# A small piece of w_q on 24 partitions in place of 16, and the last eight steps of w_o in their own order

## The chip, the cores and the metric

The kernel runs on one core of a Trainium2 chip. The metric is the time of one execution on the device, in microseconds (us). A core has TensorE (PE; its weight loads are listed apart as PEld), VectorE (DVE), ScalarE (ACT), GpSimd (POOL), SyncE (SP, which here only issues transfers), and 16 DMA engines that carry every transfer between HBM and the on-chip memory.

## The reference

One decode step of a transformer block for two tokens (B = 2, D = 448), everything in float32:

```python
xn = layernorm(x)
q  = xn @ wq                                  # 448 x 4096: 16 heads of 256
s  = softmax(q k^T / 16) v                    # 8 KV heads x 2 batches, 4096 cached positions each
s  = s.reshape(B, 1, 4096) @ wo               # 4096 x 448
g  = silu(((xn @ w_gate) * (xn @ w_up)) @ w_down)
out = x + s * g
```

The caches are 134 MB and the weights about 24 MB; each byte is read once, and there are only two tokens to use it on.

## The kernel before, in words

**Streaming.** A (KV head, batch) pair is one step i = 0..15. Its keys are a [128, 8192] float32 array and so are its values, 4 MB each. `issue` (L63 to L81) sends loads in a fixed order on SP's queue, and the order was laid down by the `plan` calls (L86 to L94): w_q's first half, k0, then for each step a pair "values of step i, keys of step i+1" (8 MB), with the other weights between them. Keys and values go to a ring of two 8 MB buffers, weights to one slot. SP waits until the buffer to be overwritten has been used, so the ring holds TensorE and the DMA queue together.

**Computing.** For step i, `values` (L282) multiplies the probabilities with v_i, `scores` (L238) makes the scores of step i+1, `softmax` (L258) turns them into probabilities. TensorE uses its array as four column blocks of 32, so that one matmul has 32 output rows and four run side by side. Float32 matmuls show as two records each in the profile, and as many weight loads.

**w_q's short end.** D = 448 is 3 x 128 + 64. The first three blocks of 128 rows are full. Of the last 64 rows, half of the columns lie on partitions 64 to 127 of the slot's block 12 (L184), and the other half is a separate array, `wqx`: 64 rows of 2 x 512 columns. Before, it is folded into 4 groups (NK) of 16 rows (SIDE), so it sits on 16 partitions with 4096 columns each, 256 KB. In HBM the 16 rows are 4 groups of 4 with an unused fifth row behind each group (L431). `rows` multiplies group j with `xeT[:, j]`, the matching 16 rows of the transposed x (L138 to L141, L178 to L181).

**The end of the kernel.** The output projection has 32 steps of 128 rows of w_o. 24 of them come earlier as a weight. The last 8 (LATE = 24) lie behind the last values in the array `last1`, in the order `THIRD` = 24, 25, 26, 28, 29, 30, 31, 27. `plan` at L94 cuts this array into eight transfers: 4096, 3072 and 1024 columns of v15, then w_o steps as 3 + 3 + 1 + 1/2 + 1/2 (a step is 448 columns; 224 KB over 128 partitions). Steps 24 to 27 multiply `oT1`, which is ready early; steps 28 to 31 multiply `oT2`, which exists only when the last two steps' outputs have been scaled (L390), combined (L391) and turned (L392). `project_last` (L323) does one step as four matmuls of 112 columns; step 27 is done in two halves of 56 columns, one per transfer. Then VectorE multiplies by the gate and adds x (L398, L399), and SP stores the result (L400).

Of the kernel before, what the change touches and what calls it, by code (L numbers as in the profile page):

```python
# [13 lines left out]
B, D = 2, 448  # L14
HKV, REP, SK, DH = 8, 2, 4096, 256
F = 1792
NT = 4
W = 32
DUP = W // 2
NK = 4  # L20
FC = F // NT
KB = 16
ROW = 8192
SL = D // NT
NC = HKV * 4
EARLY = 16
LATE = 24
THIRD = [24, 25, 26, 28, 29, 30, 31, 27]
PART = 14 * (D + 512)
SIDE = 16  # L30
EXTRA = 8
EPS = 1e-5


# [5 lines left out]
def gated_decode_block(ctx: ExitStack, tc: tile.TileContext, x, first, vk, last0, last1, wq0, wqx, wdq, wo, wgu, out):  # L40
    nc = tc.nc
# [11 lines left out]
    def bank(name=None):  # L53
        return psum.tile([128, 512], F32, name=name, bufs=1) if name else two()[:, 0]
# [4 lines left out]
    LAST = N - B  # L59
    loaded = {}  # L60
    todo = []

    def issue(n=1):  # L63
        for names, src, cuts in todo[:n]:
            weight = names[0].startswith("w")
            if weight:
                t = slot.tile([128, PART], F32, name="slot", align_bytes=512)
            else:
                t = ring.tile([128, 2 * ROW], F32, name="ring", align_bytes=512)
            width = ROW if not weight else src.shape[1] // len(names)  # L70
            for i, name in enumerate(names):
                loaded[name] = t[:, i * width:(i + 1) * width]
            if names == ["wd", "wq1"]:
                loaded["wd"], loaded["wq1"] = t[:, :14 * D], t[:, 14 * D:]
            for lo, hi in zip(cuts, cuts[1:]):
                nc.sync.dma_start(t[:, lo:hi], src[:, lo:hi])  # L76
            if names == ["wq0"]:
                at = src.shape[1]
                loaded["wqx"] = t[:, at:at + EXTRA * 512]
                nc.sync.dma_start(loaded["wqx"][:SIDE], wqx[:, :4])  # L80
        del todo[:n]  # L81

    def plan(names, src, cuts=None):
        todo.append((names.split(), src, cuts or [0, src.shape[1]]))
# [6 lines left out]
        if i in weights:  # L91
            plan(*weights[i])
    plan(f"k{LAST + 1} v{LAST}", last0, [0, ROW, 2 * ROW])
    plan(f"v{LAST + 1} wo2", last1, [0, 4096, 7168, *(ROW + i * D // 2 for i in (0, 6, 12, 14, 15, 16))])  # L94
    issue(3)


# [6 lines left out]
    ident = const.tile([128, 128], F32)  # L104
# [18 lines left out]
    xn = e1[:, 1]  # L123
    nc.vector.tensor_scalar(xn[:, :D], xc, rstd, None, op0=OP.mult)
    nc.vector.tensor_scalar(xn[:, D:], xc[:, 384:], rstd, None, op0=OP.mult)
    pt = bank()
# [5 lines left out]


    oT1 = const.tile([128, 3, 2, REP, W], F32)
    xeT = oT1[:SIDE].rearrange("p g d r m -> p (g d r) m")[:, :NK]
    pt = bank()
    for j in range(NK):
        at = 384 + j * SIDE  # L138
        nc.tensor.transpose(pt[:SIDE, B * j:B * (j + 1)], xn[:, at:at + SIDE], ident[:B, :B])
    nc.vector.tensor_copy(xeT.rearrange("p k (b j) -> p k b j", b=B),  # L140
                          pt[:SIDE, :NK * B].rearrange("p (k b) -> p k b", b=B)[:, :, :, None].to_broadcast([SIDE, NK, B, DUP]))  # L141

    both = work.tile([128, D], F32, name="h")[:B, :W].rearrange("p (b j) -> p b j", b=B)
    nc.vector.tensor_copy(both, ident[:B, :B, None].to_broadcast([B, B, DUP]))
    pt = bank()
    for c in range(NT):
        nc.tensor.matmul(pt[W * c:W * (c + 1), :SL], both.rearrange("p b j -> p (b j)"), x2[:, c * SL:(c + 1) * SL],
                         start=True, stop=True)
# [18 lines left out]
    def rows(ps, w, n, extra=None):  # L167


        def block(i):  # L170
            return w[:, i * n:(i + 1) * n]

        for k in range(3):
            for c in range(NT):
                nc.tensor.matmul(ps[W * c:W * (c + 1), :n], xnT[:, k, :], block(NT * k + c), start=k == 0, stop=False)  # L175
        if extra is not None:

            for j in range(NK):  # L178
                for c in range(2):
                    at = (c * NK + j) * n  # L180
                    nc.tensor.matmul(ps[W * c:W * (c + 1), :n], xeT[:, j, :], extra[:SIDE, at:at + n], start=False, stop=j == NK - 1)  # L181
                    if j == 0:
                        half = slice(64 * c, 64 * (c + 1))
                        nc.tensor.matmul(ps[W * (2 + c):W * (3 + c), :n], xnT[half, 3, :], block(12)[half], start=False, stop=True)  # L184
            return
        for c in range(NT):
            half = slice(0, 64) if c < 2 else slice(64, 128)
            nc.tensor.matmul(ps[W * c:W * (c + 1), :n], xnT[half, 3, :], block(12 + c % 2)[half], start=False, stop=True)
# [4 lines left out]
    def query(h):  # L193
        ps = bank()
        rows(ps, loaded[f"wq{h}"], 512, None if h else loaded["wqx"])
        for r in range(REP):
            nc.vector.transpose(qT[h][:, :, :, :, r, :].rearrange("p b g d j -> p (g d) b j"),  # L197
                                ps[:, r * 256:(r + 1) * 256])
# [16 lines left out]
    def ffn_in():  # L215
        pp = two()
        for i, w in enumerate(("wg", "wu")):
            rows(pp[:, i], loaded[w], FC)
        g = work.tile([128, FC], F32, name="h")
        nc.scalar.copy(g, pp[:, 0, :FC])  # L220
        h = work.tile([128, FC], F32, name="h")
        nc.vector.tensor_mul(h, pp[:, 1, :FC], g)
        nc.vector.transpose(hT.rearrange("p i m -> p (i m)"), h)
# [34 lines left out]
    def softmax(i, s, m, pT=None):  # L258
        sm = bank("sm")
        nc.tensor.transpose(sm[:1, :128], m[:, 0:1], ident)  # L260
        mx = work.tile([1, NT, W], F32, name="mx", bufs=1)
        nc.vector.tensor_reduce(  # L262
            mx, sm[:1, None, :128].rearrange("p o (c j) -> p o j c", c=NT).to_broadcast([1, NT, W, NT]),
            axis=AX.X, op=OP.max)
        nc.tensor.transpose(sm[:, 128:129], mx.rearrange("p c j -> p (c j)"), one)  # L265
        nc.vector.tensor_scalar(m[:, 1:2], sm[:, 128:129], -1.0 / 16, None, op0=OP.mult)  # L266
        p = work.tile([128, 2, 512], F32, name="p", bufs=1)
        nc.scalar.activation(p, s, AF.Exp, bias=m[:, 1:2], scale=1.0 / 16, accum_out=su[:, place(i):place(i) + 1])  # L268
        if pT is None:
            pT = work.tile([128, 2, 512], F32, name="pT", bufs=1)  # L270
        nc.vector.transpose(pT.rearrange("p h n -> p (h n)"), p.rearrange("p h n -> p (h n)"))  # L271
        return pT
# [38 lines left out]
    def turn(oT, cb, g, b, n):  # L311
        nc.vector.transpose(oT[:, g:g + n, :, :, DUP * b:DUP * (b + 1)].rearrange("p g d r j -> p (g d) r j"), cb)  # L312

    def heads(oT, i, first):
        return oT[:, i // 4 - first, i % 2, i % 4 // 2]
# [5 lines left out]
                             loaded["wo"][:, i * D:(i + 1) * D], start=i < NT, stop=i >= LATE - NT)  # L321

    def project_last(oT, first, i):  # L323

        at, last = THIRD.index(i) * D, i == THIRD[-1]
        cols = SL // 2 if last else SL
        for lo in range(0, SL, cols):
            for n in range(NT):
                nc.tensor.matmul(acc[W * n:W * (n + 1), lo:lo + cols], heads(oT, i, first),  # L329
                                 loaded["wo2"][:, at + n * cols:at + (n + 1) * cols], start=False, stop=last and lo > 0)  # L330
            at += NT * cols

    query(0)
    ob = work.tile([128, 8, 512], F32, name="ob", bufs=1)
# [4 lines left out]
    p = softmax(0, *ss)  # L339
    for i in range(LAST):  # L340
        g, b = divmod(i, B)
# [9 lines left out]
        p = softmax(i + 1, *ss)  # L351
# [19 lines left out]
    ps = [p]  # L371
# [3 lines left out]
    last = slot.tile([128, PART], F32, name="slot", align_bytes=512)  # L375
    p = softmax(LAST + 1, *ss, last[:, :1024].rearrange("p (h n) -> p h n", h=2))
    o = bank("o")
    values(LAST, ps[0], o)
    acc = bank()
# [10 lines left out]
    nc.scalar.activation(ob[:, 7], o, AF.Copy, scale=over[:, 15:16])  # L390
    cb = combine(ob[:, 7:], 1)  # L391
    turn(oT2, cb[:, :64], 0, 1, 1)  # L392
    for i in THIRD:
        project_last(*((oT2, 7) if i >= 28 else (oT1, 4)), i)

    r0 = work.tile([128, D], F32, name="h")[:, :SL]
# [55 lines left out]
```

## Time and profile before

| | us |
|---|---|
| median of 3 runs | 376.22 (376.15 to 376.42) |
| the profiled execution | 376.37 |
| its span, first to last instruction | 374.6 |
| DMA queue of SP, share of the 16 engines over the span | 98.2% |
| TensorE busy (matmul records) | 203.6 (54%) |
| VectorE busy | 72.6 (19%) |
| mean granted TensorE clock | 0.772 |

The profile's page gives busy times, a picture of the span in 40 slices, the DMA queues, and the chain of work that ended last. The DMA share of a stretch is the mean busy share of the 16 engines, so 0.0625 is one engine working alone. A packet's bytes are put down at its start, so that a share in a short stretch can go over 1.

### The profile page before, as it was taken

To read this page: it belongs to the slowest core of one execution; us is meant where nothing else is said; L and a number is where in the kernel's file an instruction comes from. 1 tells how busy PE (TensorE), PEld (TensorE's weight loads), DVE (VectorE), ACT (ScalarE), POOL (GpSimd) and SP (SyncE) were. 2 spreads that over 40 slices of the span, in tenths; PEclk is the share of its full clock that TensorE was granted. 3 is DMA by queue.
4 is the path that set the end of the run, shared out by engine and by line. 5 is a ranking of instruction groups with operands and counts; after the bars stand their busy time and mean duration, and the time that the engine had idled before them with its cause. 6 is when DMAs were issued, how large, how long until landed. Compare 5 with 4: busy or idle time off the path is not lost.

```text
span 374.6 us, 3200 instructions
## 1 busy us (share of the span) xinstructions
PE 203.6 (54%) x1446; PEld 57.3 (15%) x1446; DVE 72.6 (19%) x121; ACT 25.3 (7%) x39; POOL 1.2 (0%) x7
## 2 busy tenths in 40 slices
PE   1796458082734090857372665721819180909785
PEld 0111112020211020212020111200202020202222
DVE  4002130104040003040404041300120312040541
ACT  1000010001020002010101010100010101010120
POOL 1000000000000000000000000000000000000000
PEclk9956598768578577696768596885867687776999
DMA  8999899999999999999999999999999999999994
GB/s 327 432 500 441 374 432 448 448 436 435 419 442 441 441 441 400 422 448 450 420 441 434 443 415 409 457 441 434 450 420 422 441 434 427 436 409 441 413 416 178
DMA packets 4356, 158.78 MB, mean 424 GB/s; under 512 B 614, under 2 KB 1000, under 8 KB 1384
## 3 DMA queue, kind: packets, MB, share of 16 engines
q1 hardware_dynamic: 4340, 158.59, 98.2%
q8 instruction: 11, 0.18, 0.2%
q14 instruction: 1, 0.01, 0.0%
q10 hardware_dynamic: 4, 0.00, 0.0%
HBM read 158.54 MB, written 0.06 MB: 423 GB/s over the span
## 4 chain that ended last, share of the span: by engine, by line
DMA 74%; PE 24%; issue 1%; SPq 0%; DVE 0%
DMA ring<-vk 66%; PE o L286 11%; PE s L247 8%; DMA ring<-last 5%; DMA slot<-wq 3%; PE s L181 2%; PE s L175 1%; PE s L184 1%; PE s L329 0%; SPq L76 0%; PE sm L279 0%; DVE h L398 0%; DVE h L399 0%
## 5 line engine op out<-in xcount | busy, mean ns | idle before, releaser
L286 PE MATMUL o<-ring,pT 128*32 128x512 f32 x480 | 87.3, 893 | 112.4 <-DMA ring<-vk 112.4
L248 DVE TENSOR_REDUCE m<-s 128x1 f32<-128x1024 f32 x16 | 19.6, 1222 | 221.9 <-PE s L247 221.9
L247 PE MATMUL s<-ring,qT 128*32 128x512 f32 x512 | 60.7, 616 | 0.9 <-PE s L181 0.9
L286 PEld LDWEIGHTS o<-ring,pT 128*32 128x32 f32 x480 | 21.7, 155 | 167.8 <-issue 154.2
L268 ACT ACTIVATE p<-s,m 128x1024 f32<-128x1024 f32 x16 | 17.8, 1113 | 293.7 <-DVE m L266 293.7
L247 PEld LDWEIGHTS s<-ring,qT 128*32 128x32 f32 x512 | 17.5, 114 | 42.3 <-issue 39.7
L271 DVE STREAM_TRANSPOSE pT<-p 128x1024 f32<-128x1024 f32 x15 | 18.7, 1245 | 21.2 <-ACT p L268 21.2
L175 PE MATMUL s<-slot,xnT 128*32 128x512 f32 (+1 forms) x96 | 14.1, 733 | 7.3 <-DMA slot<-wq 4.3
L260 PE MATMUL sm<-ident,m 128*1 128x128 f32 x16 | 4.3, 270 | 18.8 <-DVE m L248 18.8
L265 PE MATMUL sm<-one,mx 1*128 1x1 f32 x16 | 3.5, 220 | 14.6 <-DVE mx L262 14.6
L262 DVE TENSOR_REDUCE mx<-sm 1x128 f32<-1x512 f32 x16 | 10.7, 670 | 2.1 <-PE sm L260 2.1
L347 DVE COPY ob<-o 128x512 f32<-128x512 f32 x14 | 9.5, 681 | 0.0
L181 PE MATMUL s<-slot,oT 16*32 16x512 f32 x16 | 7.4, 942 | 0.0
L320 PE MATMUL wide<-slot,oT 128*32 128x448 f32 x48 | 6.6, 699 | 0.6 <-DVE oT L312 0.6
L229 PE MATMUL s<-slot,hT 128*32 128x448 f32 x28 | 4.7, 786 | 3.4 <-DMA slot<-wdq 3.4
L260 PEld LDWEIGHTS sm<-ident,m 128*1 128x1 f32 x16 | 1.3, 79 | 33.0 <-DVE m L248 32.4
L175 PEld LDWEIGHTS s<-slot,xnT 128*32 128x32 f32 x96 | 3.6, 134 | 15.2 <-issue 15.2
L295 PE MATMUL cb<-ob,add_blocks 128*32 128x64 f32 (+2 forms) x64 | 4.3, 384 | 2.4 <-DVE ob L347 1.6
L197 DVE STREAM_TRANSPOSE qT<-s 128x256 f32<-128x256 f32 x4 | 1.6, 428 | 19.4 <-PE s L181 18.4
L265 PEld LDWEIGHTS sm<-one,mx 1*128 1x128 f32 x16 | 2.2, 136 | 17.6 <-DVE mx L262 17.6
L268 ACT ACT_TABLE_LOAD x2 | 2.6, 1283 | 27.4 <-DVE m L266 25.2
L286 PE MATMUL wide<-ring,slot 128*32 128x512 f32 x32 | 4.1, 597 | 0.0
(68 smaller groups left out, 46.8 us busy)
## 6 DMA issues: line engine op xcount, KB each, us to landing
ring<-last SPq DMA_DIRECT2D x2, 4096.0 KB, 24.1
slot<-wdq SPq DMA_DIRECT2D x1, 6720.0 KB
slot<-wgu SPq DMA_DIRECT2D x1, 6272.0 KB, 30.6
slot<-wo SPq DMA_DIRECT2D x1, 5376.0 KB, 41.9
ring<-first SPq DMA_DIRECT2D x1, 4096.0 KB, 21.0
slot<-wq SPq DMA_DIRECT2D x1, 3328.0 KB, 10.7
ring<-last SPq DMA_DIRECT2D x1, 2048.0 KB, 14.1
ring<-last SPq DMA_DIRECT2D x1, 1536.0 KB
```

The lines of the kernel that those rows point to most:

```text
L175: nc.tensor.matmul(ps[W * c:W * (c + 1), :n], xnT[:, k, :], block(NT * k + c), start=k == 0, stop=False)
L181: nc.tensor.matmul(ps[W * c:W * (c + 1), :n], xeT[:, j, :], extra[:SIDE, at:at + n], start=False, stop=j == NK - 1)
L247: nc.tensor.matmul(s[W * c:W * (c + 1), h, :], q[:, d], k[:, h, d, c, :], start=d == 0, stop=d == 1)
L248: nc.vector.tensor_reduce(m[:, 0:1], s, axis=AX.XY, op=OP.max)
L260: nc.tensor.transpose(sm[:1, :128], m[:, 0:1], ident)
L262: nc.vector.tensor_reduce(mx, sm[:1, None, :128].rearrange("p o (c j) -> p o j c", c=NT).to_broadcast([1, NT, W, NT]), axis=AX.X, op=OP.max)
L265: nc.tensor.transpose(sm[:, 128:129], mx.rearrange("p c j -> p (c j)"), one)
L268: nc.scalar.activation(p, s, AF.Exp, bias=m[:, 1:2], scale=1.0 / 16, accum_out=su[:, place(i):place(i) + 1])
L271: nc.vector.transpose(pT.rearrange("p h n -> p (h n)"), p.rearrange("p h n -> p (h n)"))
L286: nc.tensor.matmul(o[W * t:W * (t + 1), :], pT[:, h, at:at + 2 * W:2], loaded[f"v{i}"][:, e * 512:(e + 1) * 512], start=e < NT, stop=e >= ...
L320: nc.tensor.matmul(wide[W * t:W * (t + 1), :D], heads(oT, i, first), loaded["wo"][:, i * D:(i + 1) * D], start=i < NT, stop=i >= LATE - NT)
L347: nc.vector.tensor_copy(ob[:, place(i) % 8], o)
```

## The change

1. SIDE goes from 16 to 24 and the number of groups from 4 to 3 (`NS`). `wqx` is read onto 24 partitions with 2 x 3 x 512 = 3072 columns each; in HBM the 24 rows are 6 groups of 4 with an unused fifth behind each. 3 x 24 = 72 rows are 8 more than there are, and these are zeros: 288 KB are read, 256 KB are used. The transposes and matmuls on it go from 4 to 3 per column half, and the copy of the transposed x from PSUM becomes two copies (24 rows x 2 groups, 16 rows x 1 group).
2. `THIRD` is gone. Steps 24 to 31 lie and are done in their own order, each as four matmuls of 112 columns, and the array is cut into 4 + 1 + 1 + 1 + 1 steps.

```diff
-THIRD = [24, 25, 26, 28, 29, 30, 31, 27]
-SIDE = 16
-EXTRA = 8
+SIDE = 24
+NS = 3
+EXTRA = 2 * NS
...
-    plan(f"v{LAST + 1} wo2", last1, [0, 4096, 7168, *(ROW + i * D // 2 for i in (0, 6, 12, 14, 15, 16))])
+    plan(f"v{LAST + 1} wo2", last1, [0, 4096, 7168, *(ROW + i * D for i in (0, 4, 5, 6, 7, 8))])
...
-    xeT = oT1[:SIDE].rearrange("p g d r m -> p (g d r) m")[:, :NK]
+    xeT = oT1[:SIDE].rearrange("p g d r m -> p (g d r) m")[:, :NS]
     pt = bank()
-    for j in range(NK):
-        at = 384 + j * SIDE
-        nc.tensor.transpose(pt[:SIDE, B * j:B * (j + 1)], xn[:, at:at + SIDE], ident[:B, :B])
-    nc.vector.tensor_copy(xeT.rearrange("p k (b j) -> p k b j", b=B),
-                          pt[:SIDE, :NK * B].rearrange("p (k b) -> p k b", b=B)[:, :, :, None].to_broadcast([SIDE, NK, B, DUP]))
+    for j in range(NS):
+        lo, hi = 384 + j * SIDE, min(384 + (j + 1) * SIDE, D)
+        nc.tensor.transpose(pt[:hi - lo, B * j:B * (j + 1)], xn[:, lo:hi], ident[:B, :B])
+    for n, lo, hi in ((SIDE, 0, NS - 1), (64 - SIDE * (NS - 1), NS - 1, NS)):
+        nc.vector.tensor_copy(xeT[:n, lo:hi].rearrange("p k (b j) -> p k b j", b=B),
+                              pt[:n, lo * B:hi * B].rearrange("p (k b) -> p k b", b=B)[:, :, :, None].to_broadcast([n, hi - lo, B, DUP]))
...
-            for j in range(NK):
+            for j in range(NS):
+                n_rows = min(SIDE, 64 - j * SIDE)
                 for c in range(2):
-                    at = (c * NK + j) * n
-                    nc.tensor.matmul(ps[W * c:W * (c + 1), :n], xeT[:, j, :], extra[:SIDE, at:at + n], start=False, stop=j == NK - 1)
+                    at = (c * NS + j) * n
+                    nc.tensor.matmul(ps[W * c:W * (c + 1), :n], xeT[:n_rows, j, :], extra[:n_rows, at:at + n],
+                                     start=False, stop=j == NS - 1)
...
     def project_last(oT, first, i):
-
-        at, last = THIRD.index(i) * D, i == THIRD[-1]
-        cols = SL // 2 if last else SL
-        for lo in range(0, SL, cols):
-            for n in range(NT):
-                nc.tensor.matmul(acc[W * n:W * (n + 1), lo:lo + cols], heads(oT, i, first),
-                                 loaded["wo2"][:, at + n * cols:at + (n + 1) * cols], start=False, stop=last and lo > 0)
-            at += NT * cols
+        for n in range(NT):
+            at = (i - LATE) * D + n * SL
+            nc.tensor.matmul(acc[W * n:W * (n + 1), :SL], heads(oT, i, first), loaded["wo2"][:, at:at + SL],
+                             start=False, stop=i == NC - 1)
...
-    for i in THIRD:
+    for i in range(LATE, NC):
         project_last(*((oT2, 7) if i >= 28 else (oT1, 4)), i)
...
-    ends = wq0[:64, 12 * 512:].reshape(NK, SIDE // 4, 4, 2, 512).transpose(1, 2, 3, 0, 4)
+    ends = np.zeros((NS * SIDE, 2, 512), np.float32)
+    ends[:64] = wq0[:64, 12 * 512:].reshape(64, 2, 512)
+    ends = ends.reshape(NS, SIDE // 4, 4, 2, 512).transpose(1, 2, 3, 0, 4)
```

More of the change, by code (lines that the diff above doesn't have):

```diff
@@ L431 @@
     wqx = np.zeros((SIDE // 4, 5, EXTRA * 512), np.float32)
-    ends = wq0[:64, 12 * 512:].reshape(NK, SIDE // 4, 4, 2, 512).transpose(1, 2, 3, 0, 4)
+    ends = np.zeros((NS * SIDE, 2, 512), np.float32)
+    ends[:64] = wq0[:64, 12 * 512:].reshape(64, 2, 512)
+    ends = ends.reshape(NS, SIDE // 4, 4, 2, 512).transpose(1, 2, 3, 0, 4)
     wqx[:, :4] = ends.reshape(SIDE // 4, 4, EXTRA * 512)
     wq0 = np.concatenate([wq0[:, :12 * 512], np.concatenate([wq0[64:, 12 * 512:13 * 512], wq0[64:, 13 * 512:]])], 1)
-    wo = np.asarray(A_wo).reshape(NC, 128, D)[[*range(LATE), *THIRD]]
-    wo[-1] = wo[-1].reshape(128, NT, 2, SL // 2).transpose(0, 2, 1, 3).reshape(128, D)
+    wo = np.asarray(A_wo).reshape(NC, 128, D)
     wo = wo.transpose(1, 0, 2).reshape(128, NC * D)
```

## The prediction

> **What bounds the kernel now.** I read the page first: the picture of the span, the queues, the chain that ended last.
>
> ```profile
> span 374.6 us, 3200 instructions
> ...
> DMA  8999899999999999999999999999999999999994
> ...
> q1 hardware_dynamic: 4340, 158.59, 98.2%
> q8 instruction: 11, 0.18, 0.2%
> q14 instruction: 1, 0.01, 0.0%
> ...
> DMA 74%; PE 24%; issue 1%; SPq 0%; DVE 0%
> ```
>
> The 16 DMA engines are full from the first slice to the last. TensorE's share of the chain is only the moment at which a ring buffer comes free; by then the next load is queued already. Nothing that makes an engine faster in the middle can help; what counts is the bytes that each of the 16 engines has to carry, since a load has landed only when the slowest engine has brought its part. So the second view is the stages at the very end.
>
> ```profile
> core 0: us, PE busy (x) PEld busy (x) DVE busy (x) ACT busy (x) POOL busy (x), PEclk, DMA share, GB/s
> 362.00:364.00 2.00, 2.00 (x28) 0.84 (x22) 0.66 (x2) 0.00 (x0) 0.00 (x0) 1.00 0.99 419
> ...
> 368.00:368.40 0.40, 0.00 (x0) 0.00 (x0) 0.00 (x0) 0.40 (x1) 0.00 (x0) 1.00 0.75 300
> ...
> 369.20:369.60 0.40, 0.40 (x20) 0.20 (x10) 0.19 (x1) 0.00 (x0) 0.00 (x0) 1.00 0.47 170
> 369.60:370.00 0.40, 0.05 (x4) 0.00 (x0) 0.00 (x0) 0.00 (x0) 0.00 (x0) 1.00 0.37 128
> 370.00:370.20 0.20, 0.08 (x4) 0.11 (x8) 0.00 (x0) 0.00 (x0) 0.00 (x0) 1.00 0.19 67
> 370.20:370.80 0.60, 0.60 (x29) 0.60 (x31) 0.00 (x0) 0.00 (x0) 0.00 (x0) 1.00 0.07 22
> 370.80:371.00 0.20, 0.20 (x18) 0.13 (x12) 0.00 (x0) 0.00 (x0) 0.00 (x0) 1.00 0.02 4
> ```
>
> Times 16, the share counts the engines still working: 12 at 368.2, 7.5 at 369.4, 6 at 369.8, 3 at 370.1, and then 1.1. From 370.2 one engine works alone: 0.07 x 16 x 0.6 = 0.67 engine-us, of which it takes 0.60, so the second-last ended at about 370.27; in the last row 0.02 x 16 x 0.2 = 0.06, so the last ends at 370.86. It is 0.59 us behind the second-last, and four engines were done before 368. The last piece of w_o waits for this one engine.
>
> **What makes the engines unequal.** All large loads cover 128 partitions and give each engine the same. Three things do not: w_q's small piece, instruction code (q8, 11 packets of 16 KB) and the table packet (q14). How many engines share the piece can be counted in its stretch, and one packet of code can be priced.
>
> ```profile
> DMA packets 54, 1.02 MB, mean 462 GB/s; under 512 B 15, under 2 KB 15, under 8 KB 15
> ## 3 DMA queue, kind: packets, MB, share of 16 engines
> q1 hardware_dynamic: 54, 1.02, 107.4%
> ...
> q8 instruction: 1, 0.02, 1.1%
> ```
>
> The first three lines are the stretch 10.3 to 12.5 us, the last one 45 to 50 us. In the first, 54 - 15 = 39 packets carry data, of 16 KB (w_q's piece) or 32 KB (the first keys): 1.02 MB is 16 and 23 of them. So the piece is 16 packets, one per partition row. An engine moves 419 / (16 x 0.99) = 26.5 GB/s (the row of 362 us), so a 16 KB packet takes 0.62 us, and 16 packets that begin inside 2.2 us are about four engines with four packets each: four groups of four rows in HBM, four engines. Each of these carries 4 x 0.62 = 2.47 us more than the rest. A code packet costs 0.011 x 16 x 5 = 0.88 us on one engine. Followed packet by packet in the records (no view prints that), code falls on eight other engines, in turn, so that some get two; four engines have neither; the last engine is one of w_q's four, and the table packet is on it too.
>
> **The change, part 1: w_q's piece.** Six groups of four rows are, by the same pattern, six engines with four packets of 12,288 B. At 26.5 GB/s that is 0.464 us each, 1.85 us per engine: 0.62 less on the four, 1.85 more on two new ones. No row shows 24 partitions; the ends are four engines with six packets (2.78 us, 0.31 more than now) and eight engines with three (1.39). I take six, for the pattern of groups.
>
> By the Trainium skill ("DMA: Bandwidth & Descriptors", section on why a DMA increments its semaphore by 16) a transfer uses the largest number up to 16 that divides the slowest dimension on both sides, and the lowest-numbered engines: 4 of 4 and 16 before, 6 of 6 and 24 after. The count before agrees with the trace; no row here can show the numbers of the engines.
>
> The last engine then ends at 370.86 - 0.62 = 370.24, level with the second-last, which has no part in w_q and stays at 370.27. If the two new engines are among those that were done before 368, they end at 368 + 1.85 = 369.85 at the latest, and nobody waits for them. So of the 0.62 us, 0.59 reaches the end.
>
> The rest of part 1 costs nothing that counts; its cover is in these rows.
>
> ```profile
> 1.18 0.78 SPq L80 DMA_DIRECT2D slot<-wqx  x1
> 2.01 0.41 SPq L76 DMA_DIRECT2D ring<-first  x1
> 2.47 0.50 SPq L76 DMA_DIRECT2D ring<-vk  x1
> ...
> 6.21 0.27 DVE L140 COPY oT<-s 16x128 f32<-16x128 f32 x1
> ...
> 7.98 0.19 DVE L165 COPY add_blocks<-rows 128x64 f32<-128x64 f32 x1
> ...
> 11.57 4.91 PE L175 MATMUL s<-slot,xnT 128*32 128x512 f32 x24 [4.31 <-DMA slot<-wq]
> ...
> 21.16 5.33 PE L181 MATMUL s<-slot,oT 16*32 16x512 f32 x12
> ...
> 33.84 0.33 SPq L76 DMA_DIRECT2D ring<-vk  x1
> ```
>
> - VectorE: two copies for one, 0.27 us becomes at most twice that. VectorE is done at 8.2 and TensorE waits for w_q until 11.5; without that cover it would be 0.27 us.
> - SP: with six groups for four the issue may go from 0.78 to 1.17 us. The first keys, queued behind it, are issued 0.4 us later, at 2.4; the 3.4 MB of w_q ahead keep the engines busy until about 10.
> - TensorE: four of 16 records at L181 go, at 5.33 / 12 = 0.44 us: 1.8 us off the first query. The next ring load is then issued at 32.1, not 33.84. No gain: by 2.97 us SP has issued 3.4 + 0.3 + 4.2 + 8.4 = 16.3 MB, at 0.424 MB per us work until about 40. For the same reason a loss here of up to 6 us would cost nothing.
> - 32 KB more are read: in the 1.85 us already.
>
> **Part 2: the tail.**
>
> ```profile
> 365.70 2.15 PE L286 MATMUL wide<-ring,slot 128*32 128x512 f32 x16
> ...
> 368.64 0.43 PE L295 MATMUL cb<-ob,add_blocks 128*32 128x64 f32 x16 [0.79 <-ACT ob L390]
> ...
> 368.89 0.76 PE L329 MATMUL s<-ring,oT 128*32 128x112 f32 x24
> 369.14 0.25 DVE L312 STREAM_TRANSPOSE oT<-cb 128x64 f32<-128x64 f32 x1 [2.94 <-PE cb L295]
> ...
> 370.12 1.40 PE L329 MATMUL s<-ring,oT 128*32 128x112 f32 x48 [0.47 <-DMA ring<-last]
> 371.59 0.28 DVE L398 TENSOR_TENSOR h<-s,gate 128x112 f32<-128x112 f32 x1 [2.20 <-PE s L329]
> ```
>
> Transfers: five pieces of w_o before and after, eight rows of each on every engine, so 40 packets per engine either way, and the same bytes, so the last byte comes at the same time. SP issues the same number, the last two still behind a wait for earlier pieces, 13 us ahead of their data.
>
> TensorE: 72 records become 64. Steps 24 to 27 go first: 32 records at (0.76 - 0.26) / 23 = 0.022 us, from 368.89 to 369.8. Their piece is 4/3 as long, but four steps of 224 KB (8 x 1792 B per engine, 0.54 us) follow it, so it is complete at 370.27 - 2.2 = 368.1. Steps 28 to 31 need the turn that ends at 369.39, and one 224 KB piece each, at 0.54 us spacing; a step takes 8 x 0.022 = 0.18. So each waits for its piece, none for the one before, and none for the turn: step 30 would be done by 370.0 if all had landed. What comes after the last byte grows: eight records of 112 columns, 7 x 0.022 + 0.26 = 0.41 us, for eight of 56. The latter lie between nothing saved and half of it (0.21); the finish at 371.56, 0.70 after the last byte, leaves 0.3 for them if a landing is seen after 0.4. I take +0.08, bounds 0 and +0.2.
>
> [...]
>
> **The sum.** -0.59 + 0.08 = -0.51 us on the profiled 376.37: 375.86. The median was 0.15 below that execution, so the forecast for the median is 376.22 - 0.51 = 375.7, 0.14% less. A measurement of this kernel tells about 0.2% (0.75 us) from no change, so this counts as within it.
>
> **Rivals.**
>
> 1. *The two new engines are ones that carry code* (slower). Of the 12 engines at work at 368.2 the eight with code end, by the shares above, between 369 and 370.27. Plus 1.85: 370.9 to 372.1, up to 1.2 us past today's 370.86, and with 0.08 up to +1.3: 376.3 to 377.5. It decides as soon as one of the two ends after 369.0 today. For it: 8 of the 12 engines outside w_q's four carry code, and no view numbers the engines. Against it: eight engines in turn look like one half of the 16, and w_q's four lie outside it, so the next two should be in their half.
> 2. *Hidden anyway*: without the profiler the last engine is not a w_q engine, or another ends at 370.8. Then only the tail's +0.08 is left: 376.3. Against: the runs lie within 0.27 us of each other.
> 3. *The split isn't six*: four engines with six packets, +0.31 + 0.08: 376.6. Against: the groups.
> 4. *More gain*: the code packets' second round falls differently once TensorE's program is 26 records shorter, and the second-last end goes too; the row of 369.6 still has six engines at work, so at most about 1.0 us: 375.2.
>
> **How the numbers follow.** Forecast 0.46 (375.3 to 376.0; 0.09 of it below 375.47), rival 1 0.28, rival 2 0.10, rival 3 0.05, rival 4 0.11. Faster by over 0.2%: 0.11 + 0.09 = 0.20; within: 0.37 + 0.10 + 0.05 = 0.52; slower: 0.28. The range must reach into rival 1 and takes its upper bound: 375.2 to 377.5.
>
> **What would show it.** In the stretch after 10.3 us, 24 packets of 12 KB within about 1.9 us. At the end, no row with a share of 0.07 lasting 0.6 us; instead three or four engines end together near 370.25, and the last L329 records are released near 370.65. Two engines alone at 371 or later would be rival 1. A wait for the turn (DVE L312) ahead of the last records, in place of the DMA, would show my tail wrong.

## The result and the profile after

| | before | after |
|---|---|---|
| median (22 executions each) | 376.30 us | 376.53 us |
| lowest, highest | 376.15, 376.68 | 376.25, 377.94 |
| profiled execution | 376.37 | 376.53 |
| its span | 374.6 | 374.7 |

The ratio is 1.0012 (95% interval 1.0007 to 1.0018): 0.12% slower, within the 0.2% named in the prediction and inside its range, but with the other sign than the forecast of 375.7. The executions fall into two groups: 16 lie between 376.25 and 376.96 (mean 376.48, 0.16 over the mean of before, 376.32), and six between 377.50 and 377.94 (mean 377.73, 1.41 over it). The kernel before has no second group. The granted clock does not tell the two groups apart: 0.744 to 0.764 in the late six, 0.740 to 0.780 in the others.

The page of the kernel after, the lines that answer to those of before:

```profile
span 374.7 us, 3175 instructions
...
DMA  8999999999999999999999999999999999999994
...
q1 hardware_dynamic: 4350, 158.62, 98.2%
q8 instruction: 11, 0.18, 0.2%
```

The engines are as full as before, and there are still 11 code packets. The last stages, in the same columns as in the prediction (the last two are the DMA share and GB/s):

```profile
369.60:370.00 0.40, 0.40 (x24) 0.28 (x12) 0.00 (x0) 0.00 (x0) 0.00 (x0) 1.00 0.44 140
370.00:370.20 0.20, 0.20 (x12) 0.10 (x8) 0.00 (x0) 0.00 (x0) 0.00 (x0) 1.00 0.19 72
370.20:370.80 0.60, 0.47 (x16) 0.22 (x16) 0.00 (x0) 0.00 (x0) 0.00 (x0) 1.00 0.14 54
370.80:371.00 0.20, 0.20 (x8) 0.00 (x0) 0.00 (x0) 0.00 (x0) 0.00 (x0) 1.00 0.00 0
```

The lone engine is gone, as forecast: 0.14 x 16 = 2.2 engines are at work from 370.2 to 370.8. But they did not end near 370.25. A row counts a packet where it begins; followed packet by packet in the records, the last one begins at 370.79 and ends at 370.87, where the last byte came at 370.86 before. So the last matmuls are released at 371.19 and not near 370.65:

```profile
371.19 0.40 PE L329 MATMUL s<-ring,oT 128*32 128x112 f32 x8 [0.16 <-DMA ring<-last]
371.66 0.27 DVE L397 TENSOR_TENSOR h<-s,gate 128x112 f32<-128x112 f32 x1 [2.26 <-PE s L329]
```

Other engines have taken the place of the one that was relieved: in the records one with two code packets ends last, and just ahead of it, at 370.73, one of w_q's six with one code packet.

Of the rest of part 1, the start of the kernel after:

```profile
1.18 0.88 SPq L80 DMA_DIRECT2D slot<-wqx  x1
...
6.50 0.30 DVE L141 COPY oT<-s 24x64 f32<-24x64 f32 x2
...
22.06 0.34 SPq L76 DMA_DIRECT2D slot<-wgu  x1
```

The issue of the piece takes 0.10 us longer, the two copies together 0.03, and the first query ends 4.5 us earlier than in the profile of before (the slot's next load was issued at 26.53 there). That is more than the 1.8 us of the prediction; the granted clock differs, too: it was 0.50 from 21.2 to 26.5 us in the profile of before and 1.00 from 20.1 to 22.1 us here. None of it is seen at the end.

### The profile page after: what moved, and what is told of

Same layout as the page of the kernel before. It is cut to its first block, busy times and chain, and to the rows that moved or that the text cites. A ratio compares the mean times of both kernels' runs of the same rounds, so it can differ in the third digit from the quotient of the medians.

```text
span 374.7 us, 3175 instructions
## 1 busy us (share of the span) xinstructions
PE 197.8 (53%) x1433; PEld 56.7 (15%) x1433; DVE 72.6 (19%) x122; ACT 25.3 (7%) x39; POOL 1.2 (0%) x7
## 4 chain that ended last, share of the span: by engine, by line
DMA 81%; PE 18%; SPq 1%; issue 0%; DVE 0%
DMA ring<-vk 69%; DMA ring<-last 11%; PE o L289 11%; PE s L250 6%; SPq L76 0%; SPq L80 0%; PE s L329 0%; DVE h L397 0%; DVE h L398 0%
## 5 line engine op out<-in xcount | busy, mean ns | idle before, releaser
L289 PE MATMUL o<-ring,pT 128*32 128x512 f32 x480 | 83.2, 856 | 117.1 <-DMA ring<-vk 117.1
L250 PE MATMUL s<-ring,qT 128*32 128x512 f32 x512 | 59.4, 604 | 0.9 <-DVE qT L200 0.9
L274 DVE STREAM_TRANSPOSE pT<-p 128x1024 f32<-128x1024 f32 x15 | 18.7, 1245 | 21.2 <-ACT p L271 21.2
L176 PE MATMUL s<-slot,xnT 128*32 128x512 f32 (+1 forms) x96 | 15.4, 795 | 6.9 <-DMA slot<-wq 4.0
L298 PE MATMUL cb<-ob,add_blocks 128*32 128x64 f32 (+2 forms) x64 | 6.0, 499 | 2.4 <-DVE ob L346 1.6
L183 PE MATMUL s<-slot,oT 24*32 24x512 f32 (+1 forms) x12 | 4.0, 596 | 0.0
```

What stands on the lines that cost most here:

```text
L250: nc.tensor.matmul(s[W * c:W * (c + 1), h, :], q[:, d], k[:, h, d, c, :], start=d == 0, stop=d == 1)
L289: nc.tensor.matmul(o[W * t:W * (t + 1), :], pT[:, h, at:at + 2 * W:2], loaded[f"v{i}"][:, e * 512:(e + 1) * 512], start=e < NT, stop=e >= ...
L298: nc.tensor.matmul(cb[W * c:W * (c + 1), :n * 64], add_blocks[:, e].rearrange("p r j -> p (r j)"), src[:, :n, e, :, c, :], start=e == 0, s ...
```

## The experiments

Theory A: one of the two new engines carries code packets, so what part 1 takes from the last engine it gives to another; code falls on that engine once in most executions and twice in some. Theory B: part 1 gains what was forecast and the order of the tail loses more. All times below are medians with the lowest and the highest, the ratios go against runs of the kernel before on the same chip.

### The tail alone

```diff
-    plan(f"v{LAST + 1} wo2", last1, [0, 4096, 7168, *(ROW + i * D // 2 for i in (0, 6, 12, 14, 15, 16))])
+    plan(f"v{LAST + 1} wo2", last1, [0, 4096, 7168, *(ROW + i * D for i in (0, 4, 5, 6, 7, 8))])
...
-    for i in THIRD:
+    for i in range(LATE, NC):
...
```

> The kernel before with part 2 alone: w_o's last eight steps in their own order, pieces of 4, 1, 1, 1, 1; w_q's piece stays on 16 partitions. Theory A (one of the two new engines carries code, so part 1 takes from the last engine what it gives to another, and part 2 costs the longer last piece): +0.1 us against before, between 0 and +0.2, and no execution over 376.8. Theory B (the order of the tail is the loss, part 1 gains its 0.5): about +0.7 to +0.9 us in every execution.

Measured: 376.47 (376.22 to 376.93, 11 executions), ratio 1.0005 (0.9997 to 1.0014). That is not told from no change, and far from B's +0.7; two executions, at 376.82 and 376.93, lie a little over A's bound of 376.8. The traces measure the tail better. Finer stages at the end, first of the kernel before, then of this one, here with VectorE's first instruction behind the last matmul:

```profile
370.80:370.90 0.10, 0.10 (x13) 0.05 (x4) 0.00 (x0) 0.00 (x0) 0.00 (x0) 1.00 0.03 9
370.90:371.00 0.10, 0.10 (x14) 0.08 (x8) 0.00 (x0) 0.00 (x0) 0.00 (x0) 1.00 0.00 0
```

```profile
370.60:370.70 0.10, 0.10 (x8) 0.00 (x0) 0.00 (x0) 0.00 (x0) 0.00 (x0) 1.00 0.01 0
370.70:370.80 0.10, 0.10 (x8) 0.00 (x0) 0.00 (x0) 0.00 (x0) 0.00 (x0) 1.00 0.00 0
...
371.45 0.27 DVE L393 TENSOR_TENSOR h<-s,gate 128x112 f32<-128x112 f32 x1 [2.29 <-PE s L325]
```

By these rows the last byte comes at 370.85 before, and VectorE starts at 371.59 (its row stands in the prediction): 0.74 us. Here it is 370.62 to 371.45: 0.83 us. The longer last piece costs 0.09 us, for a forecast of 0.08. In the records of the other traces the same stretch is 0.79 to 0.85 us with the new order and 0.70 to 0.77 with the old one, two kernels aside in which TensorE itself ends late (they come below).

### The piece on 24 partitions alone

```diff
-SIDE = 16
-EXTRA = 8
+SIDE = 24
+NS = 3
+EXTRA = 2 * NS
...
```

> The kernel before with part 1 alone: w_q's piece on 24 partitions, w_o's end in the old order. Theory A: between -0.1 and +0.3 us in most executions, because an engine that has both 1.85 us of w_q and a code packet ends where the last one ended before; and in some executions +1.2 to +1.4 us, where that engine gets a second code packet. Theory B: -0.5 us in every execution.

Measured: 376.94 (376.19 to 377.96), ratio 1.0017 (1.0008 to 1.0027). Four of 11 executions lie at 377.47 to 377.96, seven between 376.19 and 376.95, three of them over the +0.3 that A allows. Part 1 alone makes the second group, so theory B falls.

### The piece on 20 partitions

```diff
-SIDE = 16
-EXTRA = 8
+SIDE = 20
+NS = 4
+EXTRA = 2 * NS
...
```

> The kernel before with the piece on 20 partitions: 5 groups of 4 rows, 4 groups of columns per half (rows 20, 20, 20, 4), so five engines with four 16 KB packets: the four old ones as before, and one new one with 2.47 us more. Theory A has one of the two new engines free of code and the other not. If the fifth is the free one: within 0.1 us of before (it ends at about 370.1, the last at 370.86). If the fifth is the one with code: +0.6 to +0.9 us, and +2.0 in some executions. Theory B: within 0.1 us either way, unless the fifth has code.

Measured: 376.32 (376.13 to 376.89), ratio 1.0002 (0.9993 to 1.0011): the median of before, and no second group. A fifth engine with 2.47 us more delays nothing, so the fifth is free of code: in the records of its trace, too, none of w_q's five engines carries a code packet. By A it is the sixth that does.

### No change of table

The prediction put the last engine's lateness down to w_q plus "the table packet", q14.

```diff
-        nc.scalar.activation(e, y[:, :SL], AF.Sigmoid)
+        nc.vector.tensor_scalar(e, y[:, :SL], -80.0, None, op0=OP.max)
+        nc.scalar.activation(e, e, AF.Exp, scale=-1.0)
+        nc.vector.tensor_scalar(e, e, 1.0, None, op0=OP.add)
+        nc.vector.reciprocal(e, e)
```

> The kernel before with the sigmoid of the gate made from Exp (clamped at -80, plus one, reciprocal on VectorE), so that ScalarE changes no table and the table packet of 8 KB on the last engine goes. If that engine is the last because it has w_q's 2.47 us and the table packet: the lone engine at the end is gone and the time falls by 0.5 to 0.7 us, to where the engines with two code packets end. If the last engine is late for another reason: within 0.1 us. The work it adds is three VectorE instructions of about 0.27 us at a place where VectorE waits for TensorE, so it costs nothing.

Measured: 376.46 (376.38 to 376.94), ratio 1.0005 (0.9996 to 1.0014): no gain. ScalarE's only table load is now the one at the start, and the packet is there all the same (first a row of ScalarE's timeline, then the DMA queues from 120 to 130 us):

```profile
2.21 1.28 ACT L271 ACT_TABLE_LOAD   x1 [2.21 <-DMA p<-x]
```

```profile
q14 instruction: 1, 0.01, 0.2%
```

So the packet is not a table, and this kernel didn't test what the last engine loses by it. The records show that: in all 14 traces of this case the q14 packet lies on one of w_q's engines. It takes 0.31 us, and the data packet beside it 2.95 us instead of 2.42, so this engine's data comes 0.8 us later. In the profile of the kernel without the table change 2.1 engines (0.13 x 16) end together:

```profile
370.20:370.80 0.60, 0.60 (x28) 0.60 (x32) 0.00 (x0) 0.00 (x0) 0.00 (x0) 1.00 0.13 45
370.80:371.00 0.20, 0.20 (x21) 0.18 (x12) 0.00 (x0) 0.00 (x0) 0.00 (x0) 1.00 0.02 4
```

This is the kernel before with w_q on 16 partitions and nothing added to any engine's load; here the last engine has company where in the profile of before it was alone. In the records the one with q14 ends at 370.68, and an engine with two code packets at 370.86. With the tail alone, where w_q's piece is unchanged as well, the gap is 0.23 us (370.63 behind 370.40). The gap of 0.59 us behind the second-last belonged to one execution.

### More code packets, and fewer

Does the second group come from code on the sixth engine? Code packets can be added without touching a load: TensorE gets tiny matmuls while it waits for values. In the first try (e5 and e6 in the texts below) they also stood in the last of the 14 steps.

```diff
         p = softmax(i + 1, *ss)
+        spare = bank("sm")
+        for _ in range(24):
+            nc.tensor.matmul(spare[:W, 256:258], ident[:, :W], ident[:, :2], start=True, stop=True)
```

> The kernel before (piece on 16 partitions), with 24 tiny matmuls added to TensorE in each of the 14 steps while it waits for values: 336 x 4 = 1344 more instructions, so about 16 code packets of 256 instructions in place of 11. Theory A (code packets go in turn over eight engines that do not include the four of w_q, and the sum on one engine decides): every one of the eight now has two, which three of them had already; the four of w_q are not touched. So 0 to +0.4 us against before, and no execution over 377.0. If code packets cost by their number, on whatever engine: +0.5 us or more.

> The piece on 24 partitions (w_o's end in the old order) with the same 336 tiny matmuls. Theory A (one of the two new engines is one of the eight that carry code; it has one packet in most executions and two in some): with 16 packets it has two in every execution, so all of them lie where only some lie now, at +1.2 to +1.7 us against before. If the slow executions come from something else than code on that engine: a mixture as with 11 packets, +0.1 to +0.6 in most and +1.3 in some.

Measured: 376.81 (376.60 to 378.35) on 16 partitions, with three of ten executions over 377.0 that A forbids, and 379.21 (377.66 to 379.61) on 24. These two settle nothing: in the last step the tiny matmuls lie on the chain that ends the kernel. In the profile of the first, the scores that wait behind them start late, and TensorE runs on when the loads are through:

```profile
352.29 1.95 PE L354 MATMUL sm<-ident 128*32 128x2 f32 x47 [0.25 <-DVE m L266]
354.05 1.08 PE L247 MATMUL s<-ring,qT 128*32 128x512 f32 x3
```

(The second starts at 352.26 before.) The pair was repeated with 26 matmuls in each of the first 13 steps and none in the last.

```diff
+        if i < LAST - 1:
+            spare = bank("sm")
+            for _ in range(26):
+                nc.tensor.matmul(spare[:W, 256:258], ident[:, :W], ident[:, :2], start=True, stop=True)
```

> As e5, but the tiny matmuls stand in the first 13 steps only (26 each, 338 in all), not in the last one, where e5 and e6 put them on the chain that ends the kernel. 16 code packets, two on each of the eight engines. Theory A: 0 to +0.4 us against before, no execution over 377.0, since the four engines of w_q carry no code.

> The piece on 24 partitions with the same 338 tiny matmuls in the first 13 steps. Theory A: the one new engine that carries code has two packets in every execution, so all of them lie at +1.1 to +1.6 us against before. If the late executions of 24 partitions have another cause: a mixture as without the matmuls, most within +0.6.

Measured on 16 partitions: 376.52 (376.32 to 376.85, 10 executions), ratio 1.0004 (0.9995 to 1.0014). On 24: 377.65 (377.49 to 377.87, 7 executions), ratio 1.0033 (1.0021 to 1.0044). All executions on 24 partitions are now late, none on 16 is. Both have the first of these lines on their page; the others are the end on 24 partitions, where one engine (0.07 x 16 = 1.1) works alone from 371 on:

```profile
q8 instruction: 16, 0.26, 0.2%
...
371.20:371.60 0.40, 0.18 (x8) 0.21 (x12) 0.00 (x0) 0.00 (x0) 0.00 (x0) 1.00 0.07 25
371.60:372.00 0.40, 0.40 (x25) 0.40 (x21) 0.00 (x0) 0.00 (x0) 0.00 (x0) 1.00 0.07 22
```

In the records this engine is the only one of w_q's six with code; it has two packets and ends at 372.12.

The other direction leaves out work on TensorE (half the features in all scores, half the values in 14 steps), so that the code shrinks to seven packets:

```diff
-            for d in range(2):
+            for d in range(1):
...
-        values(i, p, o)
+        values(i, p, o, 0, KB // 2)
...
```

> The piece on 24 partitions with TensorE's work cut: scores use only the first 128 of the 256 features of a head in all steps, and the first 14 steps multiply only the first half of the probabilities with the values. All loads stay. About 2000 TensorE instructions, so 7 code packets: no engine has two. Theory A: no execution over 376.9, the time within -0.5 to +0.2 us of before. If the slow executions come from something else: some of them stay near +1.3 us.

Measured: 376.24 (375.57 to 376.44, 10 executions), ratio 0.9996 (0.9986 to 1.0005). Its page counts the code:

```profile
q8 instruction: 7, 0.11, 0.1%
```

The second group is gone; one execution is at 375.57, below the -0.5 that A allows, as if the sixth engine had no packet in it (no trace shows that execution). With 16 packets all executions are late, with 11 some are, with seven none: what makes them late is how often code falls on one engine, and only where w_q's piece lies on it too.

### The piece on 32 partitions

```diff
-SIDE = 16
-EXTRA = 8
+SIDE = 32
+NS = 2
+EXTRA = 2 * NS
...
```

> The piece on 32 partitions: 8 groups of 4 rows, 2 groups of columns per half, so eight engines with four packets of 8 KB, 4 x 0.31 = 1.24 us each, in place of 1.85 on six. Theory A: an engine with 1.24 us and one code packet ends 0.6 us earlier than on 24 partitions, 0.3 to 0.6 before the present end, so other engines decide in most executions (-0.3 to +0.1 us against before); with two code packets +0.6 to +0.9 us. If one of the eight has code (as on 24), about 3 in 8 executions are so; if three have it, more than half.

Measured: 376.77 (375.86 to 377.19), ratio 1.0006 (0.9997 to 1.0016). Three executions at 375.86 to 375.95, one at 376.43, three near 376.8, three near 377.1. Six of ten are late, by 0.4 or by 0.75 us, which speaks for more than one of the eight engines with code. In the profile, of an execution of 377.12, about two engines work to the end together:

```profile
370.80:371.20 0.40, 0.32 (x14) 0.35 (x17) 0.00 (x0) 0.00 (x0) 0.00 (x0) 1.00 0.14 47
371.20:371.60 0.40, 0.40 (x28) 0.40 (x19) 0.00 (x0) 0.00 (x0) 0.00 (x0) 1.00 0.10 34
```

In the records these are two of w_q's eight engines, each with two code packets; the other six have none. The three early executions lie 0.4 to 0.5 us under before, more than A allows. No trace shows one of them, so what made them early stays open.

### The changed kernel twice more

> The changed kernel once more, for another trace. Theory A: either about 376.5, with two or three engines ending within 0.3 us of each other near 370.8, or about 377.7, with one engine alone for the last 1.2 us or so, ending near 372.2.

> The changed kernel once more, for another trace, as e11: either about 376.5 with two or three engines ending together, or about 377.7 with one engine alone for the last 1.2 us.

Both executions are late ones, 377.60 and 377.82. The end of the second:

```profile
369.60:370.00 0.40, 0.00 (x0) 0.00 (x0) 0.00 (x0) 0.40 (x1) 0.00 (x0) 1.00 0.20 76
...
370.80:371.20 0.40, 0.40 (x28) 0.40 (x23) 0.05 (x1) 0.00 (x0) 0.00 (x0) 1.00 0.07 27
371.20:371.60 0.40, 0.40 (x24) 0.26 (x13) 0.00 (x0) 0.00 (x0) 0.00 (x0) 1.00 0.22 63
371.60:372.00 0.40, 0.24 (x8) 0.00 (x0) 0.00 (x0) 0.00 (x0) 0.00 (x0) 1.00 0.07 27
372.00:372.20 0.20, 0.20 (x8) 0.16 (x8) 0.00 (x0) 0.00 (x0) 0.00 (x0) 1.00 0.05 18
...
q8 instruction: 1, 0.02, 16.4%
```

One engine works alone from 370.8 to about 372.16 (0.05 x 16 x 0.2 = 0.16; in the records to 372.19). The 0.22 in between is no other engine with data: the last line, the queues of 371.2 to 371.6 us, has the last code packet there, on an engine that was done. The last byte is 1.3 us behind that of before, and the time is 1.45 us over it. Followed packet by packet, the lone engine is one of w_q's six in both traces, with the second and the tenth code packet on it; in the trace of the result it is one of the last two and has the seventh alone. Where the turn starts differs from execution to execution.

Why 1.3 us, when a code packet takes 0.88? The prediction priced the packet alone. These are the DMA queues of the kernel before, its first code packet and two data packets, in windows of 0.01 us, so that 100% is 0.16 us (46.60, then 47.46 and, for comparison, 47.42):

```profile
q8 instruction: 1, 0.02, 548.8%
...
q1 hardware_dynamic: 1, 0.05, 1502.5%
...
q1 hardware_dynamic: 1, 0.05, 1158.1%
```

The code packet takes 0.88 us. The data packet that begins as it ends, on the same engine by the records, takes 2.40 us, where a packet of the same size on another engine takes 1.85. So the engine's data comes 0.88 + 0.55 = 1.4 us later. In seven traces followed for this, the delay is 1.41 to 1.43 us for each code packet ahead of 360 us; behind that, where the data packets are small or the engine is done, it is less.

## Why the prediction was wrong

- *What bounds the kernel*: right. The first query ended 4.5 us earlier and the issue of the piece took 0.10 us longer, and neither is seen at the end.
- *Six engines with four packets*: this was right. Of the stretch from 10.2 to 12.2 us of the kernel after, the count:

```profile
DMA packets 65, 1.02 MB, mean 508 GB/s; under 512 B 19, under 2 KB 19, under 8 KB 19
```

46 packets carry data, and 1.02 MB is 24 of 12 KB and 22 of 32 KB. The rule that the prediction cites from the Trainium skill ("DMA: Bandwidth & Descriptors", section on why a DMA increments its semaphore by 16) gives six, and this trace agrees.
- *"If the two new engines are among those that were done before 368"*: here the prediction failed. One of them was (20 partitions cost nothing), the other carries code. With 1.85 us and one packet it ends at 370.73, 0.1 us before the end of the relieved engine in the old kernel, and with two packets at 371.96 and 372.19 (the two late traces). This was rival 1, at a chance of 0.28, and its time of 376.3 to 377.5 holds the median; the late executions go past it, to 377.9. The argument against it, that eight engines in turn are one half of the 16, was a guess about numbers that no view gives; with 32 partitions two of w_q's eight engines carry code.
- *"A code packet costs 0.011 x 16 x 5 = 0.88 us on one engine"*: this price was too small. Its engine's data comes 1.4 us later, and the q14 packet, to which the prediction gave no price, costs 0.8. Before, the last engine had 4 x 0.61 of w_q and 0.8 of q14, 3.3 us more than an engine with neither; after, the sixth has 4 x 0.46 and 1.4 of code, 3.3 us as well. That the two are equal is chance.
- *The gain of 0.59*: even without the sixth engine it was too large, since it came from one trace: *the second-last stays at 370.27* does not hold from one execution to the next. That one has two code packets and no part in w_q. In the records the later of two such engines ended at 370.24 in the profile of before, but at 370.87 in that of the result, where it is the last of all, and between 370.40 and 371.00 in the four kernels from the tail alone to the one without the table change. That the q14 packet is a table was wrong.
- *The tail*: right, +0.09 for +0.08. All of it lies behind the last byte. The last matmuls took 0.40 us, for a forecast of 0.41, and began 0.32 us after the last byte, where the prediction took 0.4.
- *Rival 4*, a gain from fewer instructions: no. 26 records fewer left 11 code packets. The sum as it should read, for the usual execution: nothing at the last byte, since other engines end where the relieved one ended, and +0.09 from the tail; measured +0.16. With six of 22 executions 1.41 late, the mean rises by 0.5.

What stays open: the rest of the 0.16; what the q14 packet is, and why it lies on one of w_q's engines; and why the kernel without the table change lies 0.14 us over before in the median, if it does.

No version here beats the kernel before: 20 partitions equal it, and 32 are early only in the executions in which code happens to fall well.

## What to carry to other kernels

When the DMA engines are full from end to end, a load has landed only when the last of the 16 engines is through: multiply the DMA share of the last stages by 16, and ask which engines the odd, narrow transfers and the code lie on. A narrow transfer moved to other engines gives its time to those; whether that helps depends on what they carry already, and a single trace does not tell it where that differs between executions. Before building on a gap seen in one profile, take two or three profiles of the same kernel.

## What the runs showed of the hardware

The instruction code of TensorE is a load like any other: 11 packets of 16 KB, in turn over eight of the 16 engines. A packet takes 0.88 to 0.97 us, and the data packet beside it 0.46 to 0.55 us longer, so its engine falls behind by 1.4 us. The code goes up to 16 packets with 338 more matmuls and down to seven with a third of the matmuls left out, and on an engine that is late already a second packet costs the whole kernel 1.3 us. That the place of the packets differs between executions of one program was not expected; it makes two groups of times out of a kernel whose work is fixed.
